# A pre-norm linear-attention and gated-MLP block: the weight fold of the start rebuilt on DMA transposes and masks, its first loads spread over two queues

## The chip, the cores and the metric

The kernel runs on one core of one Trainium2 chip. A core has TensorE (PE, matrix products; its weight loads are listed apart as PEld), VectorE (DVE), ScalarE (ACT), GpSimd (POOL) and SyncE (SP). Each works through its own list of instructions in order, and they meet by semaphores. Sixteen DMA engines move data; a transfer is issued by an instruction on some engine's queue. The metric is device microseconds of one execution; lower is better.

## The reference, cut to what matters

A block on x of 2048 rows by 640 columns, bf16. Layer norm, q, k, v by one 640 x 1920 matrix, 32 heads of 20 columns; per head a small 20 x 20 matrix `w_phi` gives features, softmaxed with both signs; linear attention; output product; residual; second layer norm; gated MLP with 1536 inner columns; residual.

```python
qkv = (x @ wqkv).reshape(B, S, 3, H, Dh)           # x is already layer-normed
pq = einsum("bhsd,hdf->bhsf", q, w_phi); pk = einsum("bhsd,hdf->bhsf", k, w_phi)
phi_q = concat([softmax(pq), softmax(-pq)]); phi_k = concat([softmax(pk), softmax(-pk)])
kv = einsum("bhsf,bhsd->bhfd", phi_k, v);  z = einsum("bhsf->bhf", phi_k)
o = einsum("bhqf,bhfd->bhqd", phi_q, kv) / (einsum("bhqf,bhf->bhq", phi_q, z)[..., None] + 1e-6)
h = x + o @ wo
h2 = h + ((layernorm(h) @ w_gate) * (layernorm(h) @ w_up)) @ w_down
```

## The kernel before

The rows are cut into 16 tiles of 128 (`t`), the 640 columns into 5 chunks of 128 (`c`, `i`). Everything is listed as operations with the engine, an assumed cost and the buffers read and written. A planner (`schedule`, L741) walks through them and puts each engine's list in order; the table `TUNED` (from L48) gives each operation a due time, which is its rank in its engine's list, and a `:1` there picks the second engine that the operation allows. `emit` (L858) turns dependences into semaphore waits. So the order within each engine is fixed when the program is built, and an instruction whose input is late holds up all that stand behind it on that engine.

**Stages.** First a start, up to about 17 us, in which weights are folded and the first tiles are normed. Then the K/V stage over all tiles: V and K products (L506), exponentials (L527), row sums (L530), reciprocal (L533), a product on GpSimd (L535), and the 20-wide outer products (L544). Then Q (L565), the attention numerators (L598), output product (L641), second norm, gate and up products (L683), down product (L702), and stores (L716). From the end of the start on, TensorE's list is almost without gaps.

**The fold.** `w_phi` acts on each head of q and k, so the kernel multiplies it into the weights: K is then one product of the normed rows with a folded Wk. For this Wk has to lie with its columns on partitions. In the kernel before this is done thus:

- Wk is loaded by rows (`wk0`, `wk2`, `wk4`, L285) into `wkn`. TensorE turns it, 6 windows of at most 128 columns (starts in `WIN`) for each of 5 row chunks (`WT0` to `WT4`, L403), each followed by an eviction from PSUM (`WTe`) into `wkT`. The windows begin at multiples of 120 so that six whole heads stand on 120 partitions.
- `w_phi` is loaded with a head on each of 32 partitions (`w32`). TensorE turns it by 40 small products (`PH`, L365), an eviction (`PHd`) makes `phid`, 14 more products with a shifted identity `es` spread it over the six places of a window (`PS`, L385), and an eviction (`PHe`) makes `Phi`.
- The fold of row chunk `i` is 7 products (`F1_i`, L424) over 640 columns in all, and an eviction (`Fe1_i`) into the K part of `Wp`. The same for Wq, which is turned by six DMA transposes (`wqt`, L302) and folded later (`F0_i`).

**The first tiles.** For a tile: x load (L275), two statistics instructions and an aggregate on VectorE (L440 to L443, `L1s`, `L1a`), logarithm and exponential on ScalarE for the deviation (L448, L451), the scaled copy `xn` (L474 on ScalarE, L476 on VectorE), its transpose, then V and K. Tiles in `TPE` (0, 1, 2) are turned by TensorE (`xt`, L485) and evicted (`xte`); all others by DMA (L493). The helper `copy` (L239) records all evictions. Tiles 0 and 1 (`TSPLIT`) have their K and V in five pieces, one for each chunk of the weight, with other work between.

**Queues.** Every DMA is issued by SP. ScalarE begins with a table load (L1031). TensorE begins with 8 products on zeros (`warm`, L349), and has two more after `PH`. GpSimd builds the identity, the head masks `GL` (L328, L331), the ones in `va` (L334) and two copies (L337, L339). `GL` holds for each column of a chunk and each head that this chunk meets (7, 7, 8, 7, 7) a 1 where the column belongs to that head.

Of the kernel before, what the change touches and what calls it, by code (L numbers as in the profile page):

```python
# [17 lines left out]
H = 32  # L18
# [17 lines left out]
WIN = [0, 120, 240, 360, 480, 520]  # L36
# [4 lines left out]
TPE = (0, 1, 2)  # L41
TSPLIT = (0, 1)
NWARM = 10
# [5 lines left out]
x0:0.7 wk0:3.58 wk2:2.62 wk4:2.14 x1:1.66 wv0:4.06 wv2:4.54 wv4:5.5 x2:3.1 x4:5.98 x6:5.02 w32:1.18 x8:16.362 x10:22.358 x12:22.838 x14:23.318  # L49
wqt0:25.018 wqt1:26.238 wqt2:38.209 wqt3:39.429 wqt4:40.649 wqt5:36.989 wo0:51.098 wo2:51.578 wg0:50.618 wu0:48.218 wg1:52.058 wu1:50.138 wg2:49.178  # L50
wu2:48.698 wg3:53.018 wu3:52.538 wg4:47.738 wu4:49.658 id0:1.4 gl0:1.15 eps:0.7 id1:1.92 gla0:2.32 glb0:2.76 gla4:3.2 glb4:3.64 gla1:1.7 glb1:3.86
gla2:2.54 glb2:4.08 gla3:2.98 glb3:3.42 va1:4.3 glx:5.12 kv1:5.57 zero:0.7 warm0:1.08 warm1:1.51 warm2:1.94 warm3:2.37 warm4:2.8 warm5:3.23 warm6:3.66
warm7:4.09 warm8:6.634 warm9:6.854 es0:0.9 es1:5.37 PH:4.52 PHd:6.29:1 PS:7.409 PHe:8.479 WT0:8.823 WTe0:9.428 WT1:9.158 WTe1:9.793 WT2:8.488
WTe2:9.308:1 WT3:7.074 WTe3:7.679:1 WT4:6.02 WTe4:6.693 F1_0:10.64 Fe1_0:11.405:1 F1_1:11.214 Fe1_1:12.248 F1_2:11.787 Fe1_2:12.872:1 F1_3:9.795
Fe1_3:10.782 F1_4:9.493 Fe1_4:10.158:1 L1s0:3.343 L1a0:4.343 L1s1:4.453 L1a1:5.873 L1s2:10.278 L1a2:11.278 L1s3:7.96 L1a3:9.198 L1s4:14.48 L1a4:15.829
L1s5:13.05 L1a5:14.37 L1s6:12.23 L1a6:15.3 L1s7:11.41 L1a7:15.939 L1s8:21.828 L1a8:23.108 L1s9:19.478 L1a9:21.718 L1s10:26.058 L1a10:29.088
L1s11:27.338 L1a11:28.978 L1s12:32.038 L1a12:33.818 L1s13:28.158 L1a13:33.928 L1s14:34.958 L1a14:38.018 L1s15:35.778 L1a15:38.128 L1l0:4.633 L1e0:5.063
L1l1:6.163 L1e1:6.593 L1l2:12.028 L1e2:13.495 L1n3:13.805 L1l4:16.388 L1e4:17.337 L1n4:17.647 L1n5:18.047 L1n6:18.247 L1n7:17.847 L1l8:29.984
L1e8:30.414 L1n8:30.724 L1n9:31.124 L1n10:31.324 L1n11:30.924 L1l12:38.418 L1e12:39.329 L1n12:40.975 L1n13:40.575 L1n14:41.175 L1n15:40.775 xn0:5.373
xt0:6.355 xte0:7.042:1 xn1:7.46 xt1:8.209 xte1:8.78:1 xn2:13.87 xt2:14.806 xte2:15.41:1 xn3:14.218:1 xt3:15.142 xn4:18.018 xt4:18.698 xn5:19.507:1  # L60
xt5:21.138 xn6:18.978 xt6:19.918 xn7:18.793:1 xt7:23.798 xn8:31.185:1 xt8:32.109 xn9:33.235:1 xt9:34.549 xn10:31.899:1 xt10:33.329 xn11:33.318
xt11:35.769 xn12:43.138 xt12:44.078 xn13:42.178 xt13:42.858 xn14:42.145:1 xt14:45.298 xn15:43.638 xt15:46.518 V0_0:12.361 V0_1:12.632 V0_2:12.904
V0_3:15.9 V0_4:17.802 Ve0:20.843 K0_0:13.176 K0_1:13.447 K0_2:13.719 K0_3:13.991 K0_4:14.262 Kx0_0:14.932 Kx0_1:15.765 Ks0:16.598 Kr0:18.518 Kn0:19.158
KV0:27.582 V1_0:10.097 V1_1:10.369 V1_2:10.942 V1_3:11.516 V1_4:12.089 Ve1:13.595 K1_0:14.534 K1_1:15.085 K1_2:15.357 K1_3:15.628 K1_4:16.172
Kx1_0:16.713 Kx1_1:17.547 Ks1:20.298 Kr1:22.648 Kn1:23.288 KV1:28.258 V2:16.443 Ve2:18.17 K2:18.073 Kx2_0:20.22 Kx2_1:21.467 Ks2:23.218 Kr2:26.878
Kn2:27.518 KV2:31.65 V3:20.79 Ve3:22.713 K3:19.432 Kx3_0:22.09 Kx3_1:23.337 Ks3:24.638 Kr3:32.858 Kn3:33.498 KV3:36.401 V4:28.934 Ve4:30.562 K4:22.148
Kx4_0:23.96 Kx4_1:24.793 Ks4:29.198 Kr4:34.498 Kn4:38.216 KV4:41.153 V5:30.292 Ve5:32.612 K5:26.223 Kx5_0:28.528 Kx5_1:29.361 Ks5:30.618 Kr5:34.038
Kn5:35.857 KV5:43.187 V6:24.865 Ve6:26.873 K6:23.507 Kx6_0:25.417 Kx6_1:26.25 Ks6:36.598 Kr6:38.238 Kn6:41.375 KV6:45.222 V7:32.326 Ve7:33.955
K7:33.685 Kx7_0:35.313 Kx7_1:36.146 Ks7:40.758 Kr7:42.678 Kn7:43.734 KV7:49.973 V8:37.077 Ve8:38.706 K8:35.043 Kx8_0:36.77 Kx8_1:37.603 Ks8:38.698
Kr8:40.298 Kn8:46.093 KV8:50.951 V9:45.898 Ve9:47.526 K9:38.436 Kx9_0:40.065 Kx9_1:40.898 Ks9:44.138 Kr9:45.738 Kn9:48.452 KV9:54.343 V10:55.019  # L70
Ve10:56.648 K10:41.829 Kx10_0:43.457 Kx10_1:44.291 Ks10:46.243 Kr10:47.843 Kn10:50.811 KV10:59.396 V11:39.795 Ve11:41.521 K11:43.863 Kx11_0:45.492
Kx11_1:46.325 Ks11:48.602 Kr11:50.202 Kn11:53.17 KV11:60.072 V12:56.378 Ve12:58.006 K12:51.627 Kx12_0:53.255 Kx12_1:54.088 Ks12:54.922 Kr12:56.522
Kn12:57.888 KV12:62.71 V13:48.614 Ve13:50.341 K13:47.256 Kx13_0:48.884 Kx13_1:49.718 Ks13:50.961 Kr13:52.561 Kn13:55.529 KV13:63.386 V14:52.985
Ve14:54.712 K14:57.736 Kx14_0:59.364 Kx14_1:60.198 Ks14:61.031 Kr14:62.631 Kn14:63.271 KV14:68.96 V15:64.364 Ve15:66.405:1 K15:61.05 Kx15_0:62.678
Kx15_1:63.512 Ks15:64.345 Kr15:65.945 Kn15:66.585 KV15:69.636 KVe0:71.802 KVe1:71.192 KVe2:70.582 F0_0:64.062 Fe0_0:64.634 F0_1:59.094 Fe0_1:59.666:1
F0_2:62.408 Fe0_2:63.091:1 F0_3:50.649 Fe0_3:51.221 F0_4:60.748 Fe0_4:61.32 Q0_0:66.801 Qx0_0_0:68.151 Qx0_0_1:68.667 Q0_1:71.391 Qx0_1_0:73.257
Qx0_1_1:72.74 Q0_2:70.312 Qx0_2_0:72.178 Qx0_2_1:71.661 Q0_3:65.722 Qx0_3_0:67.071 Qx0_3_1:67.588 Q0_4:67.881 Qx0_4_0:69.746 Qx0_4_1:69.23 Q1_0:86.69
Qx1_0_0:88.556 Qx1_0_1:88.039 Q1_1:84.253 Qx1_1_0:86.118 Qx1_1_1:85.602 Q1_2:83.173 Qx1_2_0:85.039 Qx1_2_1:84.523 Q1_3:75.318 Qx1_3_0:76.668
Qx1_3_1:77.184 Q1_4:79.591 Qx1_4_0:80.94 Qx1_4_1:81.457 Q2_0:91.242 Qx2_0_0:92.591 Qx2_0_1:93.108 Q2_1:89.473 Qx2_1_0:90.822 Qx2_1_1:91.338 Q2_2:73.894
Qx2_2_0:75.76 Qx2_2_1:75.243 Q2_3:72.47 Qx2_3_0:74.336 Qx2_3_1:73.819 Q2_4:92.321 Qx2_4_0:93.67 Qx2_4_1:94.187 Q3_0:81.749 Qx3_0_0:83.098  # L80
Qx3_0_1:83.615 Q3_1:77.477 Qx3_1_0:79.343 Qx3_1_1:78.826 Q3_2:76.398 Qx3_2_0:78.263 Qx3_2_1:77.747 Q3_3:95.103 Qx3_3_0:96.453 Qx3_3_1:96.969 Q3_4:80.67
Qx3_4_0:82.536 Qx3_4_1:82.019 wd0:98.078 wd1:98.558 wd2:97.598 wd3:99.038 N0_1:73.549 N0_0:74.973 sr0:74.164 rho0:75.588 A0:75.958 B0:76.988 dd0:78.018
rd0:78.408 o0:78.888 oT0:80.309 O0:85.332 h0:86.96 L2s0:88.012 L2a0:89.012 L2v0:89.463 L2r0:90.149 hc0:89.302 hT0:90.833 N1_1:78.556 N1_0:78.901
sr1:79.171 rho1:79.661 A1:80.031 B1:81.061 dd1:82.091 rd1:82.481 o1:82.961:1 oT1:83.873 O1:87.769 h1:89.398 L2s1:90.329 L2a1:91.477 L2v1:91.767
L2r1:92.877 hc1:91.855 hT1:92.778 N2_1:90.552 N2_0:89.128 sr2:91.167 rho2:91.657 A2:92.027 B2:93.057 dd2:94.087 rd2:94.477 o2:94.957 oT2:96.378
O2:103.423 h2:105.051 L2s2:106.113 L2a2:107.474 L2v2:107.764 L2r2:108.856 hc2:107.768 hT2:108.691 N3_1:82.828 N3_0:79.246 sr3:83.693 rho3:84.183
A3:84.553 B3:85.583 dd3:86.613 rd3:87.712 o3:88.192 oT3:89.613 O3:93.4 h3:95.028 L2s3:96.09 L2a3:97.1 L2v3:97.39 L2r3:98.13 hc3:97.789 hT3:99.518
N4_1:94.758 N4_0:90.897 sr4:95.78 rho4:96.91 A4:97.28 B4:98.31 dd4:99.34 rd4:100.079 o4:100.559 oT4:101.98 O4:112.711 h4:114.869 L2s4:116.471
L2a4:117.501 L2v4:117.791 L2r4:118.363 hc4:117.791 hT4:119.043 N5_1:104.781 N5_0:105.126 sr5:105.803 rho5:107.284 A5:107.654 B5:108.986 dd5:110.188
rd5:110.749 o5:111.229 oT5:112.65 O5:117.329 h5:118.958 L2s5:119.889 L2a5:120.889 L2v5:121.179 L2r5:121.679 hc5:121.179:1 hT5:121.859 N6_1:100.003  # L90
N6_0:100.894 sr6:100.731 rho6:101.509 A6:101.879 B6:103.081 dd6:104.111 rd6:104.501 o6:104.981 oT6:106.402 O6:122.638 h6:124.679 L2s6:127.033
L2a6:128.673 L2v6:128.963 L2r6:130.533 hc6:129.103:1 hT6:129.783 N7_1:138.304 N7_0:138.649 sr7:139.193 rho7:140.121 A7:140.491 B7:141.521 dd7:142.551
rd7:142.941 o7:143.421:1 oT7:144.333 O7:154.338 h7:155.966 L2s7:156.898 L2a7:158.469 L2v7:158.759 L2r7:159.969 hc7:159.469:1 hT7:160.149 N8_1:122.293
N8_0:121.948 sr8:122.969 rho8:123.459 A8:123.829 B8:125.431 dd8:128.783 rd8:129.603 o8:130.083 oT8:132.223 O8:142.232 h8:144.153 L2s8:145.558
# [119 lines left out]
def pool_c(n):  # L214
    return 0.183 + 0.0017 * n
# [10 lines left out]
def build_graph():  # L226
# [84 lines left out]
    for g in range(6):  # L311
        PACE[7 + g // 2].append(wqt(g, 10 * (7 + g // 2) - 19))
# [100 lines left out]
    def fold(kind, i, key, eng):  # L413
        w = "wkT" if kind == 1 else "wqT"
        b = Buf("pf%d_%d" % (kind, i), "psum", 2)
        def f(e):
            first = [True, True]
            for (g, a0, a1) in FOLD:
                for (p0, p1) in ((a0, min(a1, 320)), (max(a0, 320), a1)):
                    if p1 <= p0:  # L420
                        continue
# [643 lines left out]
```

## Time and profile before

Five runs without a profile: 283.86 to 285.52 us, median 285.22. The profiled execution took 285.25 us; its span, which all times below refer to, is 283.5 us.

| Row | Value |
|---|---|
| Profiled execution, span | 285.25 us, 283.5 us |
| VectorE, ScalarE, GpSimd busy | 180.1, 106.6, 64.5 us |
| Last matmul ends, by the chain | 281.12 us |
| First V product starts | 12.06 us |
| First Q product starts | 68.75 us |
| Longest wait of TensorE after the start | 0.62 us, at 41.20 us, for a transposed tile |
| DMA moved from 2 to 12 us | about 2.9 MB |

How to read it: a group or a row of the timeline names the line of the kernel, the engine, the operation, and output and input by the program's names. In the chain of waits each row is a stretch of the work that ended last: start, length, what. In the rows by stretches of time each engine has its busy time and, in brackets, its instructions. The page rates TensorE's granted clock at 1.00 in all stretches.

### The profile page before, as it was taken

What the parts mean: (1) busy time and instruction counts of PE and PEld (TensorE: products, weight loads), DVE (VectorE), ACT (ScalarE), POOL (GpSimd) and SP (SyncE); (2) the same over time, 40 slices, a digit from 0 to 9 for tenths busy, and PEclk for the clock granted to TensorE, in tenths of its full rate; (3) what the DMA queues carried; (4) which work ended last, traced back from release to release, by engine and by line L of the source; (5) the groups of instructions that cost most, each with busy time, mean ns of one, the idle gap of its engine ahead of it and who ended that gap; (6) DMA issues with size and microseconds to landing.
All of it is one profiled execution on the core that took longest, in us unless ns stands there. A gap on an engine that the chain in (4) does not pass through costs nothing.

```text
span 283.5 us, 5153 instructions
## 1 busy us (share of the span) xinstructions
PE 278.1 (98%) x2122; PEld 185.9 (66%) x2139; DVE 180.1 (64%) x366; ACT 106.6 (38%) x188; POOL 64.5 (23%) x81
## 2 busy tenths in 40 slices
PE   8999999999999999999999999999999999999996
PEld 4877867787555588774455674554777445588774
DVE  4799999547377888787287862557867106523422
ACT  3799767555777652101323001323100203332100
POOL 5026599966011222122002001000222000000000
DMA  6628589892011596151211031011223400100111
GB/s 200 222 69 165 123 111 130 226 392 91 2 23 23 72 263 127 30 95 46 49 23 34 14 94 46 0 27 23 49 69 72 69 0 0 27 0 2 46 32 62
DMA packets 44216, 22.33 MB, mean 79 GB/s; under 512 B 35328, under 2 KB 42912, under 8 KB 44192
## 3 DMA queue, kind: packets, MB, share of 16 engines
q1 hardware_dynamic: 44192, 21.99, 33.2%
q8 instruction: 17, 0.28, 0.4%
q14 instruction: 7, 0.06, 0.1%
HBM read 11.00 MB, written 2.62 MB: 48 GB/s over the span
## 4 chain that ended last, share of the span: by engine, by line
PE 95%; DMA 2%; ACT 1%; issue 1%; DVE 0%; DVEq 0%
PE ps L683 36%; PE ps L702 18%; PE ps L506 13%; PE ps L641 8%; PE ps L565 8%; PE ps L598 4%; PE ps L544 3%; DMA xnT<-xn 2%; PE ps L349 1%; PE ps L424 1%; ACT xn L474 1%; PE ps L403 1%; ACT ev L239 1%; PE ps L365 1%; PE ps L485 0%
## 5 line engine op out<-in xcount | busy, mean ns | idle before, releaser
L683 PE MATMUL ps<-xnT,Wgu 128*128 128x512 bf16 (+1 forms) x588 | 105.7, 335 | 0.6
L683 PEld LDWEIGHTS ps<-xnT,Wgu 128*128 128x128 bf16 x600 | 58.3, 98 | 42.7 <-DVE ev L691 0.4
L688 ACT ACTIVATE scratch<-ps 128x512 bf16<-128x512 f32 (+1 forms) x60 | 30.6, 513 | 123.9 <-PE ps L683 114.8
L691 DVE TENSOR_TENSOR ev<-ps,scratch 128x512 bf16<-128x512 f32 (+1 forms) x60 | 32.9, 574 | 44.5 <-PE ps L683 26.7
L702 PE MATMUL ps<-Wp,ev 128*128 128x320 bf16 (+2 forms) x396 | 53.7, 295 | 0.0
L702 PEld LDWEIGHTS ps<-Wp,ev 128*128 128x128 bf16 x396 | 38.1, 98 | 14.1
L506 PE MATMUL ps<-Wp,xnT 128*128 128x320 bf16 x320 | 46.1, 299 | 0.6 <-DMA xnT<-xn 0.6
L535 POOL TENSOR_TENSOR ev<-ev,SR 128x1280 bf16<-128x1280 bf16 x16 | 37.4, 2360 | 10.9 <-DVE SR L533 9.1
L506 PEld LDWEIGHTS ps<-Wp,xnT 128*128 128x128 bf16 x320 | 30.4, 98 | 11.9 <-DMA xnT<-xn 1.0
L630 POOL TENSOR_TENSOR scratch<-scratch,sm 128x640 bf16<-128x640 f32 x13 | 16.5, 1272 | 67.5 <-DVE sm L627 61.9
L714 DVE SCALAR_TENSOR_TENSOR Wp<-ps,rs,x_all 128x640 bf16<-128x640 f32 (+3 forms) x18 | 14.6, 809 | 22.6 <-PE ps L702 22.4
L530 DVE TENSOR_REDUCE SR<-ev 128x64 f32<-128x1280 bf16 x16 | 23.5, 1477 | 4.3 <-ACT ev L527 3.6
L574 ACT ACTIVATE eqT<-ps 128x512 bf16<-128x512 f32 x40 | 21.7, 595 | 9.4 <-PE ps L565 9.4
L641 PE MATMUL ps<-Wo,scratch 128*128 128x320 bf16 x160 | 24.0, 299 | 0.0
L527 ACT ACTIVATE ev<-ps 128x640 bf16<-128x640 f32 x32 | 20.9, 706 | 8.1 <-PE ps L506 6.7
L565 PE MATMUL ps<-xnT,Wp 128*128 128x512 bf16 x96 | 22.5, 379 | 0.2
L655 POOL TENSOR_SCALAR ln<-mv 128x1 f32<-128x1 f32 x16 | 3.4, 210 | 83.5 <-DVE mv L654 74.4
L641 PEld LDWEIGHTS ps<-Wo,scratch 128*128 128x128 bf16 x160 | 15.5, 98 | 7.5 <-DMA scratch<-scratch 0.5
L645 DVE TENSOR_TENSOR x_all<-ps,x_all 128x640 bf16<-128x640 f32 x16 | 13.2, 822 | 7.4 <-PE ps L641 7.3
L565 PEld LDWEIGHTS ps<-xnT,Wp 128*128 128x128 bf16 x100 | 9.5, 98 | 9.6 <-DVE KVm L551 0.2
L598 PE MATMUL ps<-KVm,eqT 128*128 128x154 bf16 (+1 forms) x192 | 15.2, 221 | 0.0
L598 PEld LDWEIGHTS ps<-KVm,eqT 128*128 128x128 bf16 x192 | 12.8, 98 | 3.5
(63 smaller groups left out, 208.6 us busy)
## 6 DMA issues: line engine op xcount, KB each, us to landing
out_dram<-Wp SPq DMA_DIRECT2D x15, 160.0 KB, 1.8
x_all<-in_A_x_dram SPq DMA_DIRECT2D x7, 320.0 KB, 4.4
Wgu<-in_B_w_gate_dram SPq DMA_DIRECT2D x5, 384.0 KB, 6.2
Wgu<-in_B_w_up_dram SPq DMA_DIRECT2D x5, 384.0 KB, 5.2
Wp<-in_B_w_down_dram SPq DMA_DIRECT2D x4, 480.0 KB, 5.5
scratch<-in_A_wqkv_dram SPq DMA_DIRECT2D x2, 320.0 KB, 4.9
Wp<-in_A_wqkv_dram SPq DMA_DIRECT2D x2, 320.0 KB, 6.4
Wo<-in_A_wo_dram SPq DMA_DIRECT2D x1, 480.0 KB, 7.3
```

The costliest lines, as they stand in the source:

```text
L506: ins = e.matmul(pb(b, hb)[:, 0:320], lhsT=T["xnT"][:, NC - 1 - c, P * t:P * (t + 1)], rhs=T["Wp"][:, kind, c, 320 * hb:320 * (hb + 1)], s ...
L527: G.op("act", "Kx%d_%d" % (t, s), lambda e, s=s, b=b, ek=ek: e.activation(out=T["ek"][:, ek.slots[0], s, :].rearrange("p (b n) -> p b n", ...
L530: G.op("dve", "Ks%d" % t, lambda e, ek=ek, sr=sr: e.tensor_reduce(out=T["SR"][:, sr.slots[0], 0, :], in_=T["ek"][:, ek.slots[0], :, :].rea ...
L535: G.op("pool", "Kn%d" % t, lambda e, ek=ek, sr=sr: e.tensor_tensor(out=T["ek"][:, ek.slots[0], :, :].rearrange("p s (h f) -> p (s h) f", f ...
L565: ins = e.matmul(pb(b)[:, 0:n], lhsT=T["Wp"][:, 0, i, P * c:P * (c + 1)], rhs=T["xnT"][:, NC - 1 - i, o0:o0 + n], start=(i == 0), stop=(i ...
L574: G.op("act", "Qx%d_%d_%d" % (q, c, s), lambda e, s=s, c=c, o0=o0, n=n, b=b: e.activation(out=T["eqT"][:, s, c, o0:o0 + n], in_=pb(b)[:, 0 ...
L598: ins = e.matmul(pb(b, y)[:, 22 * h0:22 * (h0 + j1 - j0)], lhsT=T["eqT"][:, s, c, P * t:P * (t + 1)], rhs=T["KVm"][:, OFF[s, c] + j0:OFF[s ...
L641: ins = e.matmul(pb(b, hb)[:, 0:320], lhsT=T["oT"][:, oT.slots[0], c, :], rhs=T["Wo"][:, c, 320 * hb:320 * (hb + 1)], start=(c == 0), stop ...
L683: ins = e.matmul(pb(b)[:, 0:n], lhsT=T["Wgu"][:, gu, c, P * ft:P * (ft + 1)], rhs=T["xnT"][:, NC - 1 - c, o0:o0 + n], start=(c == 0), stop ...
L688: G.op("act", "g%d_%d" % (bi, ft), lambda e, pg=pg, gt=gt, n=n: e.activation(out=T["gt"][:, gt.slots[0], 0:n], in_=pb(pg)[:, 0:n], func=AF ...
L691: o_ = G.op("dve", "u%d_%d" % (bi, ft), lambda e, pu=pu, gt=gt, hh=hh, ft=ft, n=n: e.tensor_tensor(out=T["hh"][:, hh.slots[0], ft, 0:n], i ...
L702: ins = e.matmul(pb(b, hb)[:, 0:w], lhsT=T["hh"][:, hh.slots[0], ft, P * tt:P * (tt + 1)], rhs=T["Wd"][:, ft, c0 + w * hb:c0 + w * (hb + 1 ...
```

## The change

- **Wk** is no longer loaded by rows. Five DMA transposes on SP (`wk0` to `wk4`), one for each 128 rows, write `wkT` directly. `wkn`, the 30 transposes on TensorE and their evictions are gone.
- **`w_phi`** is loaded with its 640 rows on partitions, 5 chunks of 20 columns (`w5`). Three instructions `Ph0` to `Ph2` multiply it under the mask `GL` into `Phi`: for each chunk, the rows of `w_phi` once for each head that the chunk meets. In the table `Ph0` and `Ph1` are on GpSimd, `Ph2` on VectorE. `PH`, `PS`, `es`, `phid` and their evictions are gone. GpSimd's mask instructions get an earlier place, the identity a later one.
- **Fold**: chunks of 128 columns in place of windows of 120, so 6 products over 720 columns in place of 7 over 640. Wq's transposes go from six to five.
- **Loads**: tile 1, Wv's first two loads and tiles 2 and 3 are issued from ScalarE's queue, Wv's last load by SP.
- **Order**: V of tiles 0 and 1 comes ahead of K and of most folds. Tile 3 is turned on TensorE too. There are 14 warm-up products in place of 10, all ahead of the first transpose. The cost that the planner assumes for an early DMA transpose changes, and the whole table of due times is new.

```diff
-TPE = (0, 1, 2)
+TPE = (0, 1, 2, 3)
-NWARM = 10
+NWARM = 14
...
+x0:0.7 wk0:4.58 wk1:1.66 wk2:3.36 wk3:6.28 wk4:7.98 x1:0.7 wv0:1.18 wv2:2.14 wv4:2.88:1 x2:1.66 x4:7.5 x6:5.8 w5:1.18 x8:9.2 x10:19.229 x12:26.289
...
+warm7:4.09 warm8:4.52 warm9:4.74 warm10:4.96 warm11:5.18 warm12:5.4 warm13:5.62 Ph0:7.23 Ph1:6.775 Ph2:7.066:1 F1_0:11.16 Fe1_0:12.054:1 F1_1:8.672
+Fe1_1:9.257 F1_2:11.475 Fe1_2:12.677:1 F1_3:12.555 Fe1_3:13.3 F1_4:14.597 Fe1_4:15.182:1 L1s0:4.206 L1a0:5.206 L1s1:3.343 L1a1:5.026 L1s2:7.666
...
     xload("sp", 0, 1, -100)
+    for i in range(NC):
+        G.op("sp", "wk%d" % i, lambda e, i=i: e.dma_start_transpose(
+            out=T["wkT"][:, :, P * i:P * (i + 1)],
+            in_=T["A_wqkv"][P * i:P * (i + 1), D:2 * D]), 1.22, 2.6, [], [wkt_b[i]], key=-99 + i, dma=-1)
+    xload("act", 1, 2, -95, also=["sp"])
     for n_, (a, b_) in enumerate(((0, 2), (2, 4), (4, 5))):
-        dma("sp", "wk%d" % a, lambda a=a, b_=b_: T["wkn"][:, a:b_, :],
-            lambda a=a, b_=b_: T["A_wqkv"][P * a:P * b_, D:2 * D].rearrange("(c p) n -> p c n", p=P), 164 * (b_ - a),
-            wkn_b[a:b_], key=-99 + n_)
...
+        dma("act", "wv%d" % a, lambda a=a, b_=b_: T["Wp"][:, 2, a:b_, :],
...
+    xload("act", 2, 4, -93, also=["sp"])
+    xload("sp", 4, 6, -92, also=["act"])
+    xload("sp", 6, 8, -91, also=["act"])
+    dma("sp", "w5", lambda: T["w5"][:, :, :], lambda: T["A_wphi"].rearrange("h d f -> (h d) f").rearrange("(c p) f -> p c f", p=P), 160,
+        [w5_b], key=-100.5)
...
+    for k, (c0, c1) in enumerate(((0, 2), (2, 3), (3, 5))):
+        def ph(e, eng, c0=c0, c1=c1):
+            n, o0, o1 = c1 - c0, OFF[0, c0], OFF[0, c1 - 1] + NH[c1 - 1]
+            return e.tensor_tensor(
+                out=T["Phi"][:, o0:o1, :].rearrange("p (c j) f -> p c j f", c=n),
+                in0=T["w5"][:, c0:c1, :].unsqueeze(2).to_broadcast([P, n, NH[c0], DH]),
+                in1=T["GL"][:, o0:o1].rearrange("p (c j) -> p c j", c=n).unsqueeze(3).to_broadcast([P, n, NH[c0], DH]), op=ALU.mult)
+        n_ = DH * sum(NH[c0:c1])
+        G.op("pool", "Ph%d" % k, ph, pool_c(n_), LP, [w5_b] + gl_b[c0:c1], [phi_b[k]], -95, alts=[("dve", 0.065 + n_ / 960.0, LD)])
...
+    FOLD = []
+    for c in range(NC):
+        lo, hi = CH[c][0], CH[c][0] + NH[c]
+        FOLD += [(c, lo, a, min(b, hi)) for a, b in ((lo, 16), (max(lo, 16), hi)) if a < min(b, hi)]
...
+            for (c, lo, a, b_) in FOLD:
+                hb = a // 16
+                ins = e.matmul(pb(b, hb)[:, DH * (a - 16 * hb):DH * (b_ - 16 * hb)], lhsT=T[w][:, c, P * i:P * (i + 1)],
+                               rhs=T["Phi"][:, OFF[0, c] + a - lo:OFF[0, c] + b_ - lo, :].rearrange("p h f -> p (h f)"),
+                               start=first[hb], stop=True, skip_group_check=True)
...
-            G.op("pe", "xt%d" % t, xt, mm_c(*[P] * 5), LT, [xb, id_b], [b], 10 * t - 20)
+            G.op("pe", "xt%d" % t, xt, mm_c(*[P] * 5), LT, [xb, id_b], [b], 10 * t - 20,
+                 before=[G.by["warm%d" % (NWARM - 1)]] if t == 0 else [])
...
-                bw = max(bw, now + 1.7) + 0.65
+                bw = max(bw, now + 1.7)
+                bw -= o.dma * (1.0 if bw < 6.2 else 0.65)
```

In the new lists TensorE has, after the warm-up: `xt1`, `xt0`, `V1_0`, `V1_1`, `F1_1`, `V0_0`, the rest of V of tiles 1 and 0, `F1_0`, `F1_2`, `xt3`, `xt2`, `F1_3`, `K1_0`, `K1_1`, `K0_0` to `K0_3`, `F1_4`, `K1_2`, `K1_3`, V of tile 3, `K1_4`, `K0_4`, then K and V of tile 2. SP has `x0`, `w5`, `wk1`, `wv4`, `wk2`, `wk0`, `x6`, `wk3`, `x4`, `wk4`, `x8`; ScalarE's queue has, behind the table load, `x1`, `wv0`, `x2`, `wv2`. VectorE begins with the statistics of tile 1, then those of tile 0.

## What the change does to the time: a prediction

> **What bounds the kernel now.** First the page's list of busy time, for the engine that sets the time:
>
> ```profile
> PE 278.1 (98%) x2122; PEld 185.9 (66%) x2139; DVE 180.1 (64%) x366; ACT 106.6 (38%) x188; POOL 64.5 (23%) x81
> ```
>
> TensorE is busy all along, so the question is which part of its 278 us is needed. The chain that ended last, in order of time (start, length, engine, line), answers it for the start:
>
> ```profile
> 1.24 3.59 PE ps L349 x8
> 4.83 1.62 PE ps L365 x40
> 6.46 0.75 PE ps L403 x6
> 7.21 0.53 PE ps L485 x5
> ...
> 8.60 0.64 PE ps L403 x6
> 9.23 1.01 PE ps L385 x14
> 10.24 0.39 PE ps L485 x5
> 10.63 1.00 PE ps L403 x18
> 11.63 0.59 PE ps L424 x14
> 12.22 0.55 PE ps L506 x4
> ```
>
> Nothing before 11.63 us but L485 (turning x) is asked for by the reference's sums: L349 warms up, L365 and L385 rearrange `w_phi`, L403 turns Wk. The first V product (L506) starts at 12.06 us. From there to 281.12 us the chain is TensorE at work, with one wait of 0.62 us and small steps of 0.05. So **the bound is the 12 us before the first V product, plus a fixed amount of matmul work.** What the change is worth is how much earlier V begins, less the work that moves behind that point, less new waits.
>
> The other engines and the DMA, by stretches of time (window and its length, then busy us of PE, PEld, DVE, ACT, POOL; clock; DMA share; GB/s):
>
> ```profile
> 2.00:12.00 10.00, 9.78 (x115) 7.25 (x115) 6.55 (x16) 4.07 (x9) 2.84 (x12) 1.00 0.90 291
> 24.00:46.00 22.00, 21.38 (x193) 16.14 (x192) 21.89 (x41) 17.42 (x30) 16.72 (x15) 1.00 0.74 134
> 46.00:62.00 16.00, 16.00 (x160) 12.58 (x159) 9.52 (x10) 9.44 (x14) 15.47 (x7) 1.00 0.95 261
> 38.00:48.00 10.00, 9.38 (x90) 7.12 (x89) 9.61 (x14) 6.90 (x12) 10.00 (x9) 1.00 0.96 117
> ```
>
> See two things: the DMA engines are already 90% busy in the start, and from 38 to 48 us, with almost nothing but transposes, they are as busy at 117 GB/s as they are at 291 with plain loads.
>
> **The change, part by part.**
>
> *Path to the first V.* It now hangs on x alone. Both x0 (SP) and x1 (ScalarE's queue) can issue at 0.79. This row gives their landing, the next the doubt:
>
> ```profile
> x_all<-in_A_x_dram SPq DMA_DIRECT2D x2, 160.0 KB, 2.4
> ...
> 0.79 1.28 ACT L1031 ACT_TABLE_LOAD   x1 [0.79 <-PEq L1050]
> ```
>
> x1 stands behind the table load. The trace shows no DMA issued by ScalarE, so its wait lies between 0 and 1.28 us. I take 0: a sequencer that has pushed an engine's instruction is free for the next (the Trainium skill, Perfetto Trace Analysis, Per-engine timelines); no run here shows it yet. Then: landed 3.2; VectorE's statistics of tile 1 and tile 0, 0.85 each (4.25 to 5.1 in the timeline); aggregate 0.2; on ScalarE two logarithms 0.3 and an exponential 0.2; `xn1` 0.6; `xt1` 0.53 at the rate of 7.21 us; its eviction, now on ScalarE, 0.7 (L239's 128x640 rows); some 0.4 for eight handovers. 3.2 + 1.7 + 0.2 + 0.8 + 0.6 + 0.53 + 0.7 + 0.4 = **8.2 us**, 3.9 earlier than 12.06. Wv's first half is issued right behind x1 and has 6 us to land.
>
> *Work that moves behind that point.* Before, two of five folds were done by 12.06. Now all five follow: a fold was 0.29 for 640 columns in 7 products, so 0.315 for 720 columns in 6; 5 x 0.315 - 3 x 0.29 = 0.71. The five folds of Wq cost 5 x 0.03 = 0.15 more. Tile 3 on TensorE adds 0.28. Sum **1.14 us**. The removed L365, L385 and L403 are not subtracted again: they lay before 12.06.
>
> *Wk by DMA.* SP's list is x0, w5, wk1, wv4, wk2, wk0, x6, wk3, x4, wk4. SP issues a transpose in 1.3 us:
>
> ```profile
> 40.01 5.21 SPq L302 DMA_TRANSPOSE scratch<-in_A_wqkv_dram  x4
> ```
>
> so wk4 is issued near 9 us and, by the 3.9 us that Wq's transposes took to land, could land at 13. But the DMA engines set it later. Ahead of it lie 13 loads of 160 KB (x0 to x7 eight, Wv five), 2.13 MB, at the rate of the first window: 291 GB/s at 0.90 is 323 GB/s, 6.6 us. `w5` has 640 rows of 40 bytes: between 0.1 (its 25 KB) and 1.3 (a transpose, which also moves small pieces); I take 0.7. Five transposes. **Here rule and row part.** The row: 117 GB/s at 0.96 is 122 GB/s, 1.34 us for 160 KB; SP's spacing says 1.3. The rule (the Trainium skill, Advanced Engine Details and Errata, X-Bar Transpose) has transposes as fast as other DMAs, which would be 0.5. By the row wk4 lands at 2.0 + 6.6 + 0.7 + 6.5 = 15.8; by the rule at 11.8. The row wins: same matrix, same size.
>
> TensorE reaches `F1_4` after V of two tiles (20 x 0.136 = 2.72), four folds (1.26), `xt2` and `xt3` (0.56) and eight pieces of K (2.17): 8.2 + 6.7 = 14.9. So by the row it waits **0.9 us**, and in-order K of tile 1, V of tile 3 and all else stand behind it; by the rule nothing. Wk's other chunks come 1.3 to 1.8 us apart ahead of wk4 and are wanted at similar distances.
>
> *Phi by masks.* GpSimd's nearest row, 2.36 us for 1280 elements (L535), gives 0.5 and 0.3 us for 280 and 160, or up to 0.5 more each by the 0.43 of a 36-element copy (L337). GpSimd was through with its setup at 4.88 and `w5` lands near 4, so `Ph1` and `Ph0` end by 6.5; `Ph2` on VectorE, 0.4, behind `xn0`, near 7.5. `F1_1` wants them at 8.75: hidden, and one for one on the path if that cover goes.
>
> *Queues.* Four loads leave SP (4 x 0.46), two remain as new ones; this only lets transposes issue earlier. x4 and x6, before issued by 7 us, now land behind the transposes, near 12 to 14; VectorE wants them from 12 on. x8, which was issued at 18.17, moves ahead of that and gets some cover back. Wq's five transposes in place of six, Wo and the MLP loads feed work after 43 us: nothing on the path. ScalarE loses three evictions of Wk (0.81), Phi (0.7) and five V evictions (0.7), and gains four of x: relief. VectorE is about even.
>
> *Clock.* The page's 1.00 hides a half rate: L403 takes 0.64/6 = 0.107 us each at 8.60 but 1.00/18 = 0.056 at 10.63. Eight warm-up products, 3.59 us, had not been enough; the rate doubled only between 9.2 and 10.6. The skill (TensorE: Matmul & The Clock Gate, Part 1) asks for a whole busy window of about 3.4 us, whose place is free. Fourteen at 0.43 last up to 6.0 us, which holds a whole window in (6.0 - 3.4)/3.4, three of four places. So by the rule the rate is mostly full at 8.2; by the row of 8 products, V begins at half rate. If it stays so for 3.4 us more, 1.7 are lost, of which 0.9 lie beside the wait for wk4: net 0.8. I take full rate.
>
> **Sum.** 12.06 - 8.2 - 1.14 - 0.9 = **1.8 us**. The profiled execution took 285.25 us (span 283.5, 1.75 around it, unchanged), so 283.4; the median of the runs, 285.22, gives the same.
>
> **Rivals.**
>
> 1. *The transposes land in time* (they cost up to 1.1, or Wk's descriptors overlap the loads): no wait, 2.7 us, 282.5; and if the later order also sheds the 0.62 wait at 41 us, 281.9. For: SP issues early. Against: 0.90 and 0.96 in the DMA rows.
> 2. *The lead is handed back.* VectorE was busy 21.89 of 22 us from 24 to 46. Per tile it has 0.95 + 0.2 + 0.57 + 1.48 + 0.54 = 3.7 us against TensorE's 20 x 0.136 + 0.69 = 3.4. If tiles can't come faster, TensorE waits 1.6 us or so in that stage: 285.0. Against: it has 6.5 us of slack from 46 to 62, and TensorE waited for it nowhere in that stage.
> 3. *Slower: transposes in the start are dearer.* With p for each, wk4 lands at 9.3 + 5p, the gain is 8.3 - 5p: nothing at p = 1.66, slower by 0.86 from p = 1.84. One tile transpose among 13 (L493) took 2.06 to issue; at that price 287.2. Against: its five-fold repetition in a row is nowhere in the trace; the six from this matrix took 1.27 to 1.36.
>
> If x1 does wait 1.28 us, V begins at 9.5, `F1_4` is reached at 16.2, wk4 is there, and 1.4 us remain, 283.8: in the forecast's own range, 282.7 to 284.3.
>
> **Chances.** About 0.3%, 0.86 us, is what a measurement can tell. Forecast 0.56, rival 1 0.24, rival 2 0.12, rival 3 0.08. Faster: the first two and a quarter of rival 2, less a little, 0.82; same: the rest of rival 2, 0.10; slower: 0.08. The range 281.8 to 285.3 holds the first two with their unknown costs and most of rival 2.
>
> **What would show it.** Right: L506 starting near 8.2; L424's last group in the start waiting for a DMA, ending near 16; no L365, L385, L403; L485 or L506 at full rate by 9 us. x1's wait: the first VectorE statistics near 3.2 or near 4.5. Rival 2: waits of L506 or L544 for VectorE or GpSimd between 20 and 46 us. Rival 3: L424 waiting over 2 us. Wrong altogether: L506 starting after 10.9, where 12.06 - 1.14 leaves nothing.

## The result, and the profile after

The changed kernel takes 282.88 us (median of 43 runs, 281.94 to 285.94); the kernel before, run beside it, 285.04 (80 runs, 283.17 to 288.34). The ratio is 0.9934, with a 95% interval of 0.9919 to 0.9948: **about 1.9 us faster**, where 283.4 was forecast against 285.25. The profiled execution took 283.44 us, its span is 281.7, 1.8 less than the 283.5 before. It is one of the slower executions, 0.56 us above the median, so the times below may show more waiting than most executions have.

The page's list of busy time, and the chain that ended last in order of time (start, length, engine, line):

```profile
PE 274.5 (97%) x2038; PEld 181.7 (64%) x2054; DVE 181.2 (64%) x370; ACT 102.1 (36%) x182; POOL 61.0 (22%) x77
```

```profile
1.72 8.83 DMA scratch<-in_A_wqkv_dram
10.55 0.05 issue
10.60 0.49 PE ps L375 x6
11.09 2.17 PE ps L459 x16
13.27 0.64 PE ps L375 x12
13.91 0.67 PE ps L437 x10
14.58 0.32 PE ps L375 x6
14.90 1.63 PE ps L459 x12
16.53 0.32 PE ps L375 x6
```

(L375 is the fold, L459 the V and K products, L437 the turning of x.) TensorE is busy for 3.6 us less than before, but the chain no longer begins with TensorE: its first 8.83 us are **one DMA**, the first transposed chunk of Wk (`wk1`), from its issue to its landing. Behind it TensorE runs on without a gap of more than 0.05 us in this stretch.

The same stretch as a timeline (start, duration; in brackets the idle time before a group and what ended it):

```profile
0.82 0.41 ACTq L272 DMA_DIRECT2D x_all<-in_A_x_dram  x1
1.24 5.02 PE L347 MATMUL ps<-zero 128*128 128x512 bf16 x14 [1.24 <-DVE zero L342]
3.68 3.63 SPq L282 DMA_TRANSPOSE scratch<-in_A_wqkv_dram  x2
5.49 1.07 POOL L356 TENSOR_TENSOR Phi<-w,GL 128x160 bf16<-128x160 bf16 x2 [0.99 <-DMA w<-in_A_w_phi_dram]
7.99 2.76 SPq L282 DMA_TRANSPOSE scratch<-in_A_wqkv_dram  x1
8.37 0.70 PE L459 MATMUL ps<-Wp,xnT 128*128 128x320 bf16 x4 [0.37 <-ACT xnT L237]
10.60 0.49 PE L375 MATMUL ps<-Phi,scratch 128*128 128x140 bf16 x6 [1.53 <-DMA scratch<-in_A_wqkv_dram]
```

V begins at 8.37 us, at full rate (4 products in 0.70). After them `F1_1` waits 1.53 us for `wk1`. SP's issue of transposes is held up in part as well: two take 3.63 us and one takes 2.76, where the trace of before had 1.3 each (the first and the last take 1.30 and 1.20 here). The stretches of time show the same from the DMA's side (columns as before: after the engines the clock, DMA share, GB/s):

```profile
2.00:6.00 4.00, 4.00 (x13) 1.45 (x11) 1.92 (x6) 0.30 (x3) 2.94 (x11) 1.00 1.21 251
6.00:11.00 5.00, 2.27 (x23) 1.28 (x22) 3.39 (x9) 1.78 (x6) 0.56 (x1) 1.00 1.01 174
11.00:15.00 4.00, 4.00 (x48) 3.21 (x46) 2.78 (x6) 2.79 (x6) 0.00 (x0) 1.00 1.14 314
```

From 6 to 11 us the DMA engines are full, but they move 174 GB/s; in the same stretch of the kernel before it was 323 at a share of 0.97. That kernel had no transposes there, so the fairer comparison is experiment 10 below, with the same transfers in one queue, 255 GB/s:

```profile
6.00:11.00 5.00, 3.86 (x36) 2.82 (x37) 4.11 (x11) 2.54 (x7) 0.00 (x0) 1.00 1.08 255
```

So the **account of the spans** is: V 3.69 earlier (12.06 to 8.37); the new wait, -1.53; the old wait of 0.62 at 41 us is gone; -0.97, the remainder to the 1.81 that the spans differ by, is put down to work moved behind the first V product. (What follows the last product is 2.4 us long in both.)

### The profile page after: what moved, and what is told of

Same layout as the page of the kernel before. It is cut to its first block, busy times and chain, and to the rows that moved or that the text cites. A ratio compares the mean times of both kernels' runs of the same rounds, so it can differ in the third digit from the quotient of the medians.

```text
span 281.7 us, 4981 instructions
## 1 busy us (share of the span) xinstructions
PE 274.5 (97%) x2038; PEld 181.7 (64%) x2054; DVE 181.2 (64%) x370; ACT 102.1 (36%) x182; POOL 61.0 (22%) x77
## 4 chain that ended last, share of the span: by engine, by line
PE 95%; DMA 3%; issue 0%; SPq 0%; DVE 0%; DVEq 0%
PE ps L636 37%; PE ps L655 19%; PE ps L459 15%; PE ps L594 8%; PE ps L518 8%; PE ps L551 4%; PE ps L497 4%; DMA scratch<-in_A_wqkv_dram 3%; PE ps L375 1%; SPq L272 0%; PE ps L437 0%; DVE Wp L667 0%; DVEq L954 0%
## 5 line engine op out<-in xcount | busy, mean ns | idle before, releaser
L459 PE MATMUL ps<-Wp,xnT 128*128 128x320 bf16 x320 | 45.6, 299 | 0.4 <-ACT xnT L237 0.4
L459 PEld LDWEIGHTS ps<-Wp,xnT 128*128 128x128 bf16 x320 | 30.7, 98 | 11.8 <-issue 0.5
L583 POOL TENSOR_TENSOR scratch<-scratch,sm 128x640 bf16<-128x640 f32 x10 | 12.7, 1273 | 57.4 <-DVE sm L580 43.6
L617 ACT ACTIVATE xn<-x_all,mv 128x640 bf16<-128x640 bf16 x9 | 7.4, 827 | 26.1 <-DVE mv L607 26.0
```

The costliest lines, as they stand in the source:

```text
L459: ins = e.matmul(pb(b, hb)[:, 0:320], lhsT=T["xnT"][:, NC - 1 - c, P * t:P * (t + 1)], rhs=T["Wp"][:, kind, c, 320 * hb:320 * (hb + 1)], s ...
```

## The experiments

The planner's answer would move everywhere after an edit. So each kernel keeps the changed kernel's lists as they are, and only the named operations move (operation, queue or engine, the one that it comes behind). Times are medians; ratios are to the kernel before on the same chip, and are what is compared across chips.

**1. One queue.** ScalarE's four loads go back to SP, Wk's transposes stay.

```diff
+        rearrange_lists(G, order, [('x1', 'sp', 'x0'), ('wv0', 'sp', 'w5'), ('x2', 'sp', 'wk1'), ('wv2', 'sp', 'x2')])
```

> The changed kernel with the four loads of ScalarE's queue (x1, Wv's first two, x2) issued by SP, in the order x0, x1, w5, wv0, wk1, x2, wv2, wv4, wk2; all else as it was. Theory 'two queues hinder each other': wk1 landed only 8.8 us after its issue because its small packets shared the DMA engines with the loads of the other queue; in one queue it lands near 7, the first fold (L375) no longer waits for it, V starts near 9 since x1 and Wv come half a microsecond later, and the time is 0.7 to 1.5 us below the changed kernel. Rival 'a transpose is dear in the start, whatever the queue': wk1 lands at 10 or later again, the wait of 1.5 us stays or grows, and the time is 0 to 1 us above the changed kernel.

282.12 us (281.88 to 282.36), ratio 0.9892 [0.9848, 0.9936]. V begins at 8.44, `F1_1` doesn't wait, and the first DMA in the chain is now the last chunk:

```profile
10.80 4.18 DMA scratch<-in_A_wqkv_dram
14.98 0.05 issue
15.03 0.49 PE ps L375 x6
```

`wk1` is issued a microsecond later here (2.75 in place of 1.72) and yet is there in time, so its lateness comes with the second queue.

**2. `F1_1` behind all V of the first two tiles**, two queues kept.

```diff
+        rearrange_lists(G, order, [('F1_1', 'pe', 'V0_4')])
```

> The changed kernel with the first fold of Wk moved behind all of V of tiles 0 and 1 on TensorE. Theory 'only wk1 is late': 16 V products (2.2 us) run in the wait of 1.5 us, and the time falls by about 1.5 us. Rival 'all that was issued early is late until 10.5': Wv's second half and last part land at about the same time as wk1, TensorE waits for them instead, only 4 products move ahead, and the time falls by 0.5 us at most.

284.2 us (283.45 to 286.77), ratio 0.9960 [0.9936, 0.9984]: no faster than the changed kernel, and by all signs slower (on this chip its 22 runs begin at 283.45, where the six of experiment 9 lie between 281.87 and 283.56), although nothing stands before the fold but work that is due anyway. The chain:

```profile
2.32 7.36 DMA Wp<-in_A_wqkv_dram
9.68 0.05 issue
9.73 2.08 PE ps L459 x14
11.80 0.33 PE ps L375 x6
12.14 0.02 issue
12.16 0.70 ACT Wp L237
```

Wv's second half, a plain load, takes 7.36 us to land, so `wk1` isn't the only late one. Its lateness is not the second queue's mark alone: Wv's two large loads took 6.4 us in the median in the kernel before, on one queue without transposes, and 3.7 to 4.2 in experiments 1, 5 and 10. And the fold of `F1_0` then waits 0.9 us for the eviction of `F1_1`, since they share PSUM banks. Waiting in another place doesn't pay.

**3. Wk by rows, turned by TensorE**, with V ahead, masks and two queues kept. Five loads by rows, 25 products and five evictions in place of five transposes.

```diff
+        wk.emit = lambda e, i=i: e.dma_start(T["wkn"][:, i, :], T["A_wqkv"][P * i:P * (i + 1), D:2 * D])
+            for c in range(NC):
+                ins = e.transpose(out=bank(i)[:, P * c:P * (c + 1)], in_=T["wkn"][:, i, P * c:P * (c + 1)], identity=T["ident"][:, :])
```

> The changed kernel with one part undone: Wk comes by rows again (five loads of 160 KB on SP, Wk's last two ahead of x4 to x7) and TensorE turns it by 25 transposes, with five evictions; masks for Phi, V ahead of K and the two queues stay. Theory 'the turn by DMA is about even': TensorE has 1.4 us more to do and loses the wait of 1.5 us, so the time is within 0.6 us of the changed kernel, and what was gained came from Phi by masks and from V not waiting for the fold. Rival 'the turn by DMA is the gain': at least 1.5 us above the changed kernel.

287.13 us (286.45 to 288.16), ratio 1.0071 [1.0049, 1.0094]. This placing had a fault of its own: one eviction stood on VectorE ahead of the statistics of tiles 2 and 3 and held them up from 7.8 to 11.4 us. So it was placed anew in experiment 6.

**4. `F1_1` and `F1_0` ahead of V**, as the fold stood in the kernel before.

```diff
+        rearrange_lists(G, order, [('F1_1', 'pe', 'xt0'), ('F1_0', 'pe', 'F1_1'), ('Fe1_0', 'act', 'Fe1_1')])
```

> The changed kernel with two folds of Wk (chunks 1 and 0) put ahead of V of tiles 0 and 1 on TensorE. Theory 'V ahead of K is what covers the landing of Wk': the first V product starts near 13, behind wk0's fold, and 20 products (2.7 us) lie behind that point which lay before it: 2.2 to 2.7 us above the changed kernel, at or above the kernel before. Rival 'the order is of no account, later waits take it up': within 0.5 us.

286.7 us (284.44 to 287.78), ratio 1.0039 [1.0014, 1.0063]: by the ratios some 3 us above the changed kernel, more than was expected, from two causes. The list of TensorE's waits (sum, times, longest) has

```profile
PE ps L375 <- DMA scratch<-in_A_wqkv_dram: 2.9, 2, 2.0
```

and the chain, behind those waits,

```profile
11.90 0.76 PE ps L375 x6
12.66 4.72 PE ps L459 x20
```

20 V products in 4.72 us, 0.236 each, where they take 0.136 at full rate: 2.0 us lost, since TensorE was back at half rate after the waits (the turned tiles before them, 10 products in 0.97, are as quick as in the changed kernel; the fold behind them takes 0.76, where it takes 0.33 in experiment 2). V ahead of the folds fills the time in which Wk lands, and it keeps TensorE at full rate.

**5. One queue, and `wk1` behind `x2` and `wv2`.** It tells the queue from the order.

```diff
+        rearrange_lists(G, order, [('x1', 'sp', 'x0'), ('wv0', 'sp', 'w5'), ('x2', 'sp', 'wv0'), ('wv2', 'sp', 'x2')])
```

> Only issues move: SP has x0, x1, w5, wv0, x2, wv2, wk1, wv4, wk2, ... and ScalarE's queue has none. Wk's first transpose is thus issued behind all early loads but wv4, near 4.7 us. Theory A (loads and transposes on two queues hinder each other, in one queue they do not): wk1 lands at most 4 us after its issue, by 8.8 us, so TensorE's wait at F1_1 is under 0.4 us, and the wait moves to F1_4 (wk4 issued near 12, landing near 16, 0.8 us or so later than with wk1 ahead): median 282.1 to 283.3 us. Theory B (what counts is whether wk1 comes ahead of the loads in the order, whatever the queue): wk1 lands near 10 us again, F1_1 waits 1.2 us or more, and with wk4 late as well 283.3 to 284.5 us.

282.06 us (281.91 to 282.28), ratio 0.9895 [0.9854, 0.9935], with no wait for Wk at `F1_1` and 0.2 us or so at `F1_4`:

```profile
9.06 0.48 PE L375 MATMUL ps<-Phi,scratch 128*128 128x140 bf16 x6
```

`wk1` was issued at 3.78, two microseconds later than in the changed kernel, and was there at least 1.5 us sooner (9.06 against 10.60). Not the order, but loads on one queue beside transposes on the other, goes with the delay. `x1` shows it too: issued behind `x0` on SP, it brought the first statistics sooner (second row) than when ScalarE issued it at 0.82 in the changed kernel (first row).

```profile
3.95 0.49 DVE L392 BATCH_NORM_STATS2 st<-x_all 128x6 f32<-128x320 bf16 x1 [2.76 <-DMA x_all<-in_A_x_dram]
```

```profile
3.67 0.49 DVE L392 BATCH_NORM_STATS2 st<-x_all 128x6 f32<-128x320 bf16 x1 [2.49 <-DMA x_all<-in_A_x_dram]
```

What it is about the second queue stays open. On one queue SP's issue of a transpose also holds back the loads behind it by 1.3 us; with two they are issued meanwhile. A run with two queues and ScalarE's loads held back would tell these apart; there was none.

**6. Wk by rows again**, with evictions where they block no list.

```diff
-    for i, (pe_ref, ev, ev_ref) in ((1, ("xt0", "act", "xte0")), (2, ("V1_4", "dve", "Ph2")), ...
+    for i, (pe_ref, ev, ev_ref) in ((1, ("xt0", "act", "xte0")), (2, ("V1_4", "act", "Fe1_1")), (0, ("V0_1", "dve", "L1a3")),
+                                    (3, ("V0_3", "act", "WTe2")), (4, ("V0_4", "dve", "Ve1"))):
```

> As in the earlier run with Wk by rows and 25 products of turning on TensorE, but the evictions of the turned chunks stand where no engine's list is blocked by them early. Theory A (turning Wk on DMA is worth little by itself: it saves TensorE some 1.4 us of turning and costs a wait of 1.5 us): 282.3 to 283.7 us, no wait of TensorE for DMA, about 1.4 us more turning ahead of the last fold. Theory B (turning by DMA is a good part of the gain, since the evictions cost VectorE and ScalarE time that the first tiles need): 284.5 to 287 us, with TensorE's waits for xn, xnT or scratch in the first 20 us over 1.5 us in sum.

285.8 us (284.39 to 286.78), ratio 1.0031 [1.0010, 1.0052]. TensorE's waits:

```profile
PE ps L459 <- DMA xnT<-xn: 1.1, 1, 1.1
PE ps L437 <- DVE xn L428: 0.7, 1, 0.7
PE ps L375 <- DVE st L393: 0.3, 1, 0.3
PE ps L852 <- DMA scratch<-in_A_wqkv_dram: 0.3, 1, 0.3
```

2.4 us of waits, most of them of VectorE's making (the 0.3 put down to `st` is not: the fold doesn't read `st`, and ScalarE's eviction of the turned chunk ran until 9.24, just before the fold at 9.38). The evictions push `xn` of tiles 2 and 3, and all that VectorE has behind them, later (they begin at 13.80, in the changed kernel at 12.96), until a tile's transpose (`xnT`) comes late. With the 25 products (1.4 us at 0.056 each) that is 3.8 us in place of the wait of 1.53 in the changed kernel: 2.3 of the 2.5 us by which the span is longer. Theory A had no wait for DMA and 283.7 at most; it fell. So in this order Wk by DMA is worth 2.5 us, and without it V ahead of K gives no gain. An order planned anew for the row loads might do better; it wasn't tried.

**7. Eight warm-up products in place of 14.**

```diff
-NWARM = 14
+NWARM = 8
```

> The changed kernel with 8 warm-up products in place of 14; TensorE idles from about 5 us to the turned tile near 7.1. Theory A [...]: V of tile 1 runs at half rate, 0.27 us for 2 products in place of 0.14, and the rate doubles only some 3 to 4 us later or after the wait for wk1: 1 to 2 us slower than the changed kernel, 283.9 to 284.9 us. Theory B (8 products are enough, or the wait for wk1 covers it): within 0.4 us of the changed kernel, 282.5 to 283.3 us.

284.25 us (283.03 to 285.90), ratio 0.9993 [0.9972, 1.0014]: the whole gain is gone, some 1.7 us by the ratios. In the timeline the V products are at half rate until 13.9 us:

```profile
8.49 1.22 PE L459 MATMUL ps<-Wp,xnT 128*128 128x320 bf16 x4 [0.35 <-ACT xnT L237]
10.11 3.96 PE L459 MATMUL ps<-Wp,xnT 128*128 128x320 bf16 x16
```

V of two tiles and `F1_1` take 5.42 us (8.49 to 13.91) where they take 3.03 in experiment 5 (8.52 to 11.55), 2.4 more. But in this execution `wk1` was there when `F1_1` wanted it, at 9.51, so the wait of 1.53 fell away, and the span is only 0.8 above the changed kernel's. With two queues, then, the landing isn't the same each time.

**8. As 1, with the load of tiles 4 and 5 behind `wk4`.**

```diff
+        rearrange_lists(G, order, [('x1', 'sp', 'x0'), ('wv0', 'sp', 'w5'), ('x2', 'sp', 'wk1'), ('wv2', 'sp', 'x2'), ('x4', 'sp', 'wk4')])
```

> As the earlier run with all first loads in SP's queue behind x0, with x1, w5, wv0 ahead of wk1; besides, the load of tiles 4 and 5 (x4) moves behind wk4. Theory A (wk4 sets F1_4 and 160 KB-per-tile loads ahead of it delay it by what they weigh): wk4 is issued 0.05 to 0.5 us and lands 0.5 to 1.0 us earlier than in that run (15.0), F1_4 waits under 0.2 us, and tiles 4 and 5 are still in time: 281.2 to 281.9 us. Theory B (x4 late costs VectorE its lead in the statistics of tiles 4 and 5, or wk4 is bound by the transposes ahead of it alone): 282.0 to 283.0 us.

282.48 us (282.28 to 283.39), ratio 0.9915 [0.9886, 0.9943]: no gain on experiment 1. V began early, at 8.01, but then met Wv's second half:

```profile
9.90 2.08 PE L459 MATMUL ps<-Wp,xnT 128*128 128x320 bf16 x14 [0.59 <-DMA Wp<-in_A_wqkv_dram]
```

Why that load was later than in experiment 1, with the same issues ahead of it, stays open.

**9 and 10. The changed kernel, and experiment 5, once more on one chip.**

> The changed kernel once more, unedited. Theory A (with loads on ScalarE's queue beside transposes on SP's, Wk's landing varies from execution to execution, and the time with it): its runs spread over 2 us or more, and this profile has a wait at F1_1 that differs from 1.5 us by 0.5 us or more. Theory B (the landing is fixed, and the wait of 1.5 us is there in every execution): the wait is 1.3 to 1.7 us again. Median 282.3 to 283.5 us in both.

> One queue, with x2 and wv2 ahead of wk1, once more, beside the changed kernel on the same chip. Theory A (one queue takes the wait for wk1 away and the variation with it): 281.9 to 282.4 us, 0.5 to 1.2 us below the changed kernel's median, runs within 0.6 us. Theory B (its earlier six runs were lucky, and it is no better than the changed kernel): within 0.4 us of the changed kernel, with runs spread over 2 us.

The changed kernel: 282.64 us (281.87 to 283.56), ratio 0.9894 [0.9848, 0.9940], and in the profiled execution, the slowest of its six, the wait is 1.57 us:

```profile
10.71 0.49 PE L375 MATMUL ps<-Phi,scratch 128*128 128x140 bf16 x6 [1.57 <-DMA scratch<-in_A_wqkv_dram]
```

That is theory B's number, and the spread of 1.7 us is under theory A's 2. But the same program also ran in 281.87, and experiment 7, with the same issues, had no such wait. That it varies in the changed kernel too is likely, not shown.

One queue: 281.98 us (281.72 to 282.42), ratio 0.9870 [0.9826, 0.9914], 0.66 below the changed kernel beside it. The two intervals overlap; but experiments 1, 5 and 10 make 18 runs from 281.72 to 282.42, all below both medians of the changed kernel (282.88 and 282.64). This is the best version found. From issue to landing, Wk's transposes took in the changed kernel, and then in experiment 10:

```profile
DMA to landing us min/median/max: 3.5/7.1/8.8
```

```profile
DMA to landing us min/median/max: 3.1/3.7/4.6
```

**11 and 12. `x1` ahead of `x0`; and 12 warm-up products besides.**

```diff
+        rearrange_lists(G, order, [('x1', 'sp', 'x0'), ('x0', 'sp', 'x1'), ('wv0', 'sp', 'w5'), ('x2', 'sp', 'wv0'), ('wv2', 'sp', 'x2')])
```

> As the one-queue kernel with x2 and wv2 ahead of wk1; besides, x1 is issued ahead of x0, since VectorE takes tile 1 first. x1 lands some 0.4 us earlier, the first statistics start near 3.3 in place of 3.7. Theory A (the chain of x sets the first V product): V starts 0.3 to 0.4 us earlier, near 8.1, and the time is 281.6 to 282.0 us. Theory B (the 14 warm-up products, which end at 6.2 to 7.4 as the clock doubles late or early, set it): V starts at 8.3 to 8.6 when they end past 7, and the time is that of the one-queue kernel within 0.2 us.

> As the kernel before with x1 ahead of x0, and with 12 warm-up products in place of 14: at half rate they end by 6.4 us in place of 7.3. Theory A (warm-ups at half rate stand ahead of the first turned tile, and 12 suffice for the clock): V starts near 8.0 at full rate, 281.4 to 281.9 us. Theory B (12 do not hold the clock up through the gap ahead of the first turned tile): the first V products are at half rate, 0.24 us apart in place of 0.14, and the time is 282.5 to 283.7 us.

The first: 282.08 us (281.87 to 282.40), ratio 0.9873 [0.9829, 0.9917]. The statistics began at 3.08 in place of 3.67 (experiment 5), but the warm-up products ran until 7.25 and V began at 8.41: theory B. The second: 282.68 us (282.02 to 283.46), ratio 0.9898 [0.9847, 0.9948]. Its V began 0.9 us earlier, at full rate, and bought nothing:

```profile
7.53 0.70 PE L459 MATMUL ps<-Wp,xnT 128*128 128x320 bf16 x4 [0.37 <-ACT xnT L237]
8.77 0.49 PE L375 MATMUL ps<-Phi,scratch 128*128 128x140 bf16 x6 [0.54 <-DMA scratch<-in_A_wqkv_dram]
```

In this execution V's start was as theory A had it, the time not, and the reason is neither's: Wk's landing is reached sooner, and there the rest of the lead is spent (0.54 us here, 0.28 at `F1_4`). But it is one of the three faster runs of six (282.02 to 282.21). The other three took 283.14 to 283.46 and left no trace; that in them 12 products didn't bring full rate, which was theory B, isn't ruled out.

## Why the prediction was right, and where not

Its mechanism held: the gain is V's earlier start, less work moved, less a wait for Wk. Its sum of 1.8 us is the 1.81 of the spans, but by **errors that cancel**: the new wait was 0.63 larger than forecast, and the old one of 0.62, which the sum left in place, went. V's lateness and the work moved, 0.17 each, cancel too. That the figure fits so closely is luck.

- *V at 8.2*: 8.37. `x1` didn't wait behind the table load, as was taken: it was issued at 0.82, while the table load ran from 0.79. But the first statistics began at 3.95, where a landing at 3.2 was taken; the steps behind it took 4.4 us in place of 4.9. (The terms as written add up to 8.13, not 8.2.)
- *Work moved, 1.14*: 0.97, as the remainder of the account, not measured by itself.
- *A wait of 0.9 us at `F1_4`, for `wk4`*: **the step that failed.** The wait was at `F1_1`, for `wk1`, and 1.53; `F1_4` had none. The prediction priced `wk4` with care and passed over the others with "Wk's other chunks come 1.3 to 1.8 us apart ahead of wk4 and are wanted at similar distances". It costed transposes one after another, at the price of a stretch in which they are almost alone. Beside loads from ScalarE's queue they took 7.1 us to land in the median, 8.8 at most, and even their issue on SP was held up. Experiments 1, 5 and 10 take away the second queue, in two orders of the loads, and the wait goes. With one queue the prediction's picture is right: in experiment 1 `wk4` is the last to come, at 14.98 (it was put at 15.8), and `F1_4` waits for it, though by 0.3 us.
- *The way to `F1_4`*: miscounted. Six pieces of K stand ahead of it in the new list, not eight (the chain has them as 12 products in 1.63 us, where 2.17 was put). By its own figures `F1_4` was to be reached at 14.4 and to wait 1.4, which leaves a gain of 1.3: the slip brought the forecast nearer to the result.
- *The 0.62 wait at 41 us*: priced only in rival 1, with 281.9; it was gone in the changed kernel. What shed it wasn't tried.
- *Rule against row* for a transpose (0.5, an estimate by the rule, or 1.3 us for 160 KB; the Trainium skill, Advanced Engine Details and Errata, X-Bar Transpose): with one queue the row held, SP issuing Wk's transposes in 1.2 to 1.3 us each in experiments 1, 5 and 10. Neither foresaw the wait: what counted was not the price of one, but what was in flight beside it. The page DMA: Bandwidth & Descriptors of the same skill (Issuing engines are not separate DMA queues) has a second issuing engine save the issuing time and nothing else. Here it saved none that showed (V at 8.37 with two queues, at 8.05 to 8.52 in experiments 1, 5 and 10) and cost some 0.7 us.
- *Masks hidden*: `Ph1` and `Ph0` ended at 6.56 (6.5 forecast), `Ph2` at 7.85 (7.5), and `F1_1` came up at 9.07. Right, with 1.2 us of cover, though `w5` was there only by 5.45, where 4 was taken.
- *Clock*: full at 8.37, as taken. The other case was put at 1.7 us of loss, a net 0.8 beside a wait for Wk. In experiment 7 the loss is 0.6% of ratio, some 1.7 us, and 0.8 between the two profiled executions.
- *Rival 1*, no wait and 281.9 to 282.5, is what one queue gives. *Rival 2* fell: TensorE waits for nothing from 11 us on. *Rival 3* was near in kind, transposes dearer in the start, but it took a price for each and looked at `wk4`, whose cover was long; `wk1` has none but 4 products.

Of the change's parts, these were taken back one at a time, with the two queues kept unless named: Wk by DMA and V ahead of K carry the gain together (without one of them the time is 0.3 to 0.4% above the kernel before, in lists that weren't planned anew), eight warm-up products are too few for it, and the scalar queue takes some of it back. The masks and the turning of tile 3 on TensorE weren't taken back alone.

## What to carry to other kernels

Price every transfer at the consumer that comes first, not only the last one of a series: the earliest has the least cover. Where transposes and bulk loads must start together, try them in one queue before spreading them over two. An earlier start of a stage is worth only what the next landing allows, so after each gain in a start look again for the wait that comes next.

## What the runs showed of the hardware that was not expected

With a second queue of loads beside them the transposes were slow: their landings took 7.1 and 7.4 us in the median in the two profiles of the changed kernel, 3.7, 3.8 and 3.7 in those of experiments 1, 5 and 10, with the same bytes to move. The other traces agree: 6.5, 6.9 and 5.9 in experiments 2, 4 and 7 with two queues, 4.2, 3.8 and 4.0 in 8, 11 and 12 with one.

TensorE's rate doubles at different points in different executions. The same program (experiment 10, then experiment 5, timeline) spent on the same 14 warm-up products:

```profile
1.24 4.53 PE L347 MATMUL ps<-zero 128*128 128x512 bf16 x14 [1.24 <-DVE zero L342]
```

```profile
1.24 6.11 PE L347 MATMUL ps<-zero 128*128 128x512 bf16 x14 [1.24 <-DVE zero L342]
```

At 0.43 us each in half rate (14 in 6.11, of which the last includes its end) and 0.22 in full (24 products of this width in 5.34 later in the changed kernel), that is 7 products at half rate in the one and all 14 in the other: the doubling came 3 us after TensorE's start, or over 6. V then began at 8.05 and at 8.52. The page's granted clock is 1.00 in both, so the rate is to be read from the spacing of products. Warm-up beyond need is itself on the path when the doubling is late, by some 0.4 us here; too little of it cost 1.7 by the ratios in experiment 7.
